# Queries of a recurrent-memory attention layer: copied and turned in two pieces of eight heads

## The chip, the cores and the metric

The kernel runs on one core of a Trainium2 chip. The metric is the device time of one execution in microseconds (us): for the kernel before, the median of three runs is 1795.13 us (1789.95, 1795.13 and 1798.88). Apart from these there is one execution taken by the hardware profiler, and all durations below come from that one.

The engines are named as in the profile: PE is the matrix engine (PEld its loading of weights), DVE is VectorE, ACT is ScalarE, POOL is GpSimd, and SP is the queue that starts most DMA transfers. L909 is line 909 of the kernel file.

## The reference

An input of 2048 rows of 1024 numbers is normalised; the result is the input, plus a dense layer with a GELU, plus an attention layer that goes through the rows in 64 segments of 32 tokens and carries 8 rows of memory from each segment to the next. The second part is the one that matters here:

```python
for s in range(n_seg):                       # 64 segments, one after the other
    xs = x[:, s * seg_len:(s + 1) * seg_len, :].copy()
    h = jnp.concatenate([mem, xs], axis=1)   # 8 rows of memory + 32 tokens
    q = jnp.einsum('btd,dhe->bhte', h, Wq)   # 32 heads of 128
    k = jnp.einsum('btd,dhe->bhte', h, Wk)
    v = jnp.einsum('btd,dhe->bhte', h, Wv)
    scores = jnp.einsum('bhqe,bhke->bhqk', q, k) * scale
    scores = jnp.where(mask[None, None], scores, -1000000000.0)
    p = _softmax(scores, axis=-1)
    o = jnp.einsum('bhqk,bhke->bhqe', p, v)
    o = jnp.einsum('bhte,hed->btd', o, Wo)
    mem = o[:, :M, :].copy()                 # M = 8, for the next segment
    outs.append(o[:, M:, :])
```

A segment can't begin before the memory of the one before is there, so the 64 segments form one long chain. The four weight matrices (1024 x 4096 each, in bf16) are too large to stay on the chip beside everything else.

## The kernel before

The first 405 us or so hold the normalisation and the dense layer. Then the loop over the 64 segments runs to the end (`for s in range(NSEG)`, line 803); the change lies in this loop alone.

**Weights.** The four matrices are cut into 64 units of 128 x 2048 numbers (512 KB). 47 of them lie in SBUF for the whole loop. 17 are brought in anew in every segment, through a ring of six buffers: 15 of these by DMA from DRAM (started from SP's queue at line 284 whenever `unit_done` says that a buffer is free), and two by VectorE out of PSUM, where they are kept (line 273).

**One segment on PE.** The order of work on each engine is the order in which the program is written; nothing is rearranged. PE goes through the passes K0, Q0, K1, Q1, V0, V1 (keys, queries and values of the two halves of 16 heads) and then O, the output product. A pass is eight units, one unit is four products of 32 rows by 512 columns side by side (line 830), and its sum goes to one PSUM bank. 24 of a segment's tokens and the 8 rows of memory are the 32 rows of these products. The other 8 tokens of each of four segments are gathered to a second set of 32 rows, the "left" rows, whose extra products fall on certain passes of certain segments. So the segments come in four kinds, by s modulo 4, which the code calls `i4`; `i4` = 1 and 3 have the more PE work, `i4` = 2 the least.

**Turning the queries.** A pass of queries leaves in its PSUM bank, for each of 16 heads, blocks of 32 tokens by 32 features. `turn_q` (line 906) has ScalarE copy them to SBUF as bf16 (line 909), into `q_home`, which has 40 columns a head: 8 for the left rows and 32 for these. Then VectorE turns each 32 x 32 block in its place (line 914, in the profile STREAM_TRANSPOSE `kq<-kq`). `q_left` (line 925) puts the left rows' queries into the first 8 columns of each head. `q_home` is the first 640 columns of `q_all`, a part of the tile `kq`.

**Who needs the turned queries.** `scores(u)` (products at line 947 for the own rows, at line 953 for the left rows) takes the turned queries and keys. `scores(0)` is written into PE's order after seven units of pass K1 (after six in segments with `i4` = 3), `scores(1)` after the first unit of V1 (after the second with `i4` = 3). If the turn isn't finished when PE comes there, PE waits, as do all units behind.

**The two calls differ.** Queries of the first half (`turn_q(psQ)`, line 1130) are copied whole, 512 columns in one instruction. For the second half (`turn_q(psQ1, (0, 10, 16))`, line 1151) the copy has two pieces, heads 0 to 9 and heads 10 to 15. The reason is in `exps(0)`, line 969: the probabilities of the first half are put into columns 400 to 623 of `q_all`, which is where heads 10 to 15 lie. They are read last at line 1024, in `sums(0)`. So the copy of heads 10 to 15 has to wait for line 1024, and that of heads 0 to 9 hasn't. The turn is one instruction over all 16 heads in both calls.

On VectorE's queue the order around the second call is line 1012, line 1024 (twice), line 925, line 914. On ScalarE's queue it is line 996, line 999 (twice), line 909 (twice), and then the copy of the values, line 886.

Of the kernel before, what the change touches and what calls it, by code (L numbers as in the profile page):

```python
# [38 lines left out]
NL = SEG - NX  # L39
# [81 lines left out]
def kernel(  # L121
# [16 lines left out]
    nc = tc.nc  # L138
# [60 lines left out]
    for j in range(4):  # L199
# [11 lines left out]
        out=m, in_=m, pattern=[[1, NX]], compare_op=ALU.is_ge, fill=0.0, base=0, channel_multiplier=-1,  # L211
    )
    for half in range(2):
        m = mask_left[0:SEG, :, 8 - 8 * half:16 - 8 * half]
        nc.gpsimd.affine_select(
            out=m, in_=m, pattern=[[-8, GRP], [0, 8]], compare_op=ALU.is_ge, fill=0.0, base=0, channel_multiplier=1,
        )
        nc.gpsimd.affine_select(
            out=m, in_=m, pattern=[[8, GRP], [1 if half else 0, 8]], compare_op=ALU.is_ge, fill=0.0,
# [91 lines left out]
    nat_home, q_home = d_oL[:, 0:512].rearrange("p (h t) -> p h t", h=16), q_all[:, 0:640].rearrange("p (h t) -> p h t", h=16)  # L311
# [29 lines left out]
    def new_ps(way="ps"):  # L341
        k = turns[way][0]
        turns[way].rotate(-1)
        shape, kind = ([P, 512], F32) if way == "ps" else ([P, KT, P], BF16)
        ps = banks.tile(shape, kind, name=way, tag=f"bank{k}")
        place_of[id(ps)] = k, ps
        return ps

    with tc.tile_pool(name="ma", bufs=2) as ma:
# [31 lines left out]
        for j in range(4):  # L381
            nc.sync.dma_start(
                out=o_sb[32 * j + NX:32 * j + 32, 0:8, :],
                in_=mem0[:, 256 * j:256 * j + 256].rearrange("m (h e) -> m h e", h=8),
# [200 lines left out]
        for tg in range(4):  # L585
# [18 lines left out]
            for fb in range(FC):  # L604
                if tg == 0 and fb < BEGUN:
                    ps = begun[fb]
                else:
                    ps = new_ps()
# [3 lines left out]
                    out=xb[:, :], in_=ps[:, :], func=ACT.Identity, bias=b1col[:, fb:fb + 1], scale=1.0  # L612
# [4 lines left out]
                    out=u[:, :], in0=u[:, :], scalar1=0.044715, scalar2=1.0, op0=ALU.mult, op1=ALU.add  # L617
# [18 lines left out]
            if tg == 0:  # L636
                for nb in range(2):
                    cs = slice(nb * 512, nb * 512 + 512)
                    ps = new_ps()
# [3 lines left out]
            if not last:  # L643
# [7 lines left out]
                for t in range(4):  # L651
# [6 lines left out]
                    for nb in range(2):  # L658
                        cs = slice(nb * 512, (nb + 1) * 512)
                        ps = new_ps()  # L660
# [21 lines left out]
            else:  # L682
# [32 lines left out]
                for step in range(FC + AHEAD):  # L715
                    for t in range(4):
# [3 lines left out]
                        for nb in range(2):  # L720
# [6 lines left out]
                            if add_at.get(fc + 1) == n:  # L727
                                ps, cs = pss[n], slice(512 * nb, 512 * nb + 512)
# [7 lines left out]
    with tc.tile_pool(name="late", bufs=1) as late:  # L736
# [15 lines left out]
        def let_go(ps):  # L752
            free_banks.append(bank_of.pop(id(ps))[0])
# [49 lines left out]
        for s in range(NSEG):  # L803
# [44 lines left out]
            def half_pass(w, u, left, at):  # L848


                ps = new_acc()
                now = [i for w_, i, u_ in units[:48] if (w_, u_) == (w, u)]
                psL, ahead, order = None, [], now
                if left and led and led["next"][:2] == (w, u):
                    psL, ahead, order = led["next"][2:]
                    assert led["made"] == len(ahead)
                    led.clear()
                elif left:
                    psL = new_acc()
                lag = LAG if first else 0  # L860
                tiles = {}
                for n in range(KT + lag):
                    if n < KT:
                        tiles[now[n]] = unit_tile((w, now[n], u))
                        product(w, now[n], tiles[now[n]], hT, ps, now)
                    if n < lag:
                        continue
                    i = now[n - lag]
                    t = tiles.pop(i)
                    if left and i not in ahead:  # L870
                        product(w, i, t, hL, psL, order)
                    if first and (w, i, u) == IN_PSUM:
                        for b in range(2):
                            keep(IN_PSUM, 1024 * b, t[:, 1024 * b:1024 * b + 1024], b)
                    unit_done((w, i, u))
                    for fn in at.get(n - lag, ()):
                        fn()
                return ps, psL
# [24 lines left out]
                kL[u] = left_keys[u]  # L903
                turn(ps, kL[u], nc.vector.tensor_copy if first else nc.scalar.copy)

            def turn_q(ps, cuts=(0, 16)):

                for h0, h1 in zip(cuts, cuts[1:]):
                    nc.scalar.copy(  # L909
                        out=q_home[:, h0:h1, NL:40], in_=ps[:, 32 * h0:32 * h1].rearrange("p (h e) -> p h e", e=32)  # L910
                    )
                let_go(ps)
                home = q_home[:, :, NL:40]
                nc.vector.transpose(out=home, in_=home)  # L914

            def turn_qL(ps, u):
                turn(ps, qL[u][:, :, :], nc.vector.tensor_copy)
# [1 line left out]
            def q_left(u):  # L919

                if i4 >= 2 + u and more:
                    q = qS[:, i4 - 2 - u, :, :]
                else:
                    q = qL[u][:, :, NL * i4:NL * i4 + NL]
                nc.vector.tensor_copy(out=q_home[:, :, 0:NL], in_=q)
# [201 lines left out]
            if first:  # L1127
                turn_qL(psQL, 0)
                q_left(0)
            turn_q(psQ)  # L1130
            if left_q[0] and not first:
                turn_qL(psQL, 0)
# [14 lines left out]
            psQ1, psQ1L = half_pass("Q", 1, left_q[1], at)  # L1147
            if first:
                turn_qL(psQ1L, 1)
                q_left(1)  # L1150
            turn_q(psQ1, (0, 10, 16))
            if left_q[1] and not first:
                turn_qL(psQ1L, 1)
            if not final:
# [45 lines left out]
            for n, unit in enumerate(O_UNITS):  # L1200
# [8 lines left out]
                if n == 6 and left_o:  # L1209
                    st["resL"] = pd_main[:, 0:256]  # L1210
                    loads.dma_start(
                        out=st["resL"], in_=resL_d[og, :, :]
# [104 lines left out]
```

## Time and profile before

| what | value | from |
|---|---|---|
| median of the runs | 1795.13 us | three runs |
| the profiled execution | 1796.11 us, its span 1794.4 us | its own time |
| PE busy | 1696.3 us, 95% of the span | page, part 1 |
| DVE busy | 983.8 us, 55% | page, part 1 |
| ACT busy | 683.6 us, 38% | page, part 1 |
| one copy L909 of 512, 320, 192 columns | 586, 429, 319 ns | groups by shape |
| one turn L914 of 512 columns | 711 ns, 128 of them | groups |

How to read it: the span is the time from the first to the last instruction of the profiled execution. "Busy" is the time in which an engine had an instruction under way; the ends of PE's products are modelled, and a product of 512 columns is shown as 380 ns though the next one starts some 215 ns after it, so that a short pause of PE can hide behind the shown end of the product before. The granted clock of PE was 1.000 over the whole execution. "DMA share" is the time that packets took, summed over the 16 DMA engines and divided by 16 times the stretch; it can be a little over 1 where packets overlap.

### The profile page before, as it was taken

What the parts mean: (1) busy time and instruction counts of PE and PEld (TensorE: products, weight loads), DVE (VectorE), ACT (ScalarE), POOL (GpSimd) and SP (SyncE); (2) the same over time, 40 slices, a digit from 0 to 9 for tenths busy, and PEclk for the clock granted to TensorE, in tenths of its full rate; (3) what the DMA queues carried; (4) which work ended last, traced back from release to release, by engine and by line L of the source; (5) the groups of instructions that cost most, each with busy time, mean ns of one, the idle gap of its engine ahead of it and who ended that gap; (6) DMA issues with size and microseconds to landing.
All of it is one profiled execution on the core that took longest, in us unless ns stands there. A gap on an engine that the chain in (4) does not pass through costs nothing.

```text
span 1794.4 us, 71508 instructions
## 1 busy us (share of the span) xinstructions
PE 1696.3 (95%) x31164; PEld 889.3 (50%) x31164; DVE 983.8 (55%) x2514; ACT 683.6 (38%) x1692; POOL 300.4 (17%) x586
## 2 busy tenths in 40 slices
PE   9999999999999999999999999999999989999988
PEld 5444444444555555545454555554545544554544
DVE  7656483825555555555455555555555554555544
ACT  6344251603333333334343434343434333433333
POOL 0000002301231111212122121121121111111111
PEclk9999999999999999999999999999999999999999
DMA  9455312789999999999999999999999999999998
GB/s 279 144 169 165 87 48 73 267 277 371 391 385 383 387 376 384 377 379 382 365 394 371 390 386 398 378 393 372 374 382 384 385 371 369 380 383 381 370 386 316
DMA packets 232830, 594.44 MB, mean 331 GB/s; under 512 B 57715, under 2 KB 88035, under 8 KB 232516
## 3 DMA queue, kind: packets, MB, share of 16 engines
q1 hardware_dynamic: 197584, 567.08, 84.4%
q0 software_dynamic: 16896, 16.85, 2.9%
q10 hardware_dynamic: 18036, 5.94, 1.3%
q8 instruction: 244, 4.00, 0.9%
q14 instruction: 70, 0.57, 0.1%
HBM read 573.43 MB, written 28.90 MB: 336 GB/s over the span
## 4 chain that ended last, share of the span: by engine, by line
PE 75%; DMA 11%; ACT 4%; DVE 4%; issue 4%; ACTq 1%; SPq 1%; POOL 0%; DVEq 0%; POOLq 0%
PE acc L830 38%; PE acc L1088 12%; PE ps L534 10%; DMA u<-Wc_O 8%; PE ps L662 6%; PE ps L693 3%; DMA u<-Wc_V 2%; ACT mixed L999 2%; PE acc L1039 1%; PE mixed L947 1%; DVE kq L914 1%; ACTq L459 1%; DVE pd_main L1012 1%; ACT kq L909 1%; SPq L521 1%
## 5 line engine op out<-in xcount | busy, mean ns | idle before, releaser
L830 PE MATMUL acc<-u,hr_home 128*32 128x512 bf16 x11520 | 758.8, 380 | 14.7 <-issue 8.3
L830 PEld LDWEIGHTS <-hr_home 128*32 128x32 bf16 x12288 | 350.3, 96 | 281.1 <-issue 33.2
L830 PE MATMUL acc<-u,hrL 128*32 128x512 bf16 x2880 | 256.2, 380 | 2.6 <-DVE qL L882 1.0
L534 PE MATMUL ps<-u 128*128 128x512 bf16 (+1 forms) x992 | 195.0, 358 | 0.0
L273 DVE TENSOR_SCALAR u<-kept 128x512 uint32<-128x512 uint32 x254 | 163.2, 684 | 56.9 <-PE acc L830 43.2
L1088 PE MATMUL acc<-u,d_oL 128*32 128x512 bf16 x2592 | 168.9, 380 | 13.1 <-issue 7.9
L882 ACT CAST d_oL<-acc 128x512 bf16<-128x512 f32 x143 | 82.0, 584 | 256.8 <-PE acc L830 251.5
L1088 PE MATMUL acc<-u,kq 128*32 128x256 bf16 (+1 forms) x2884 | 135.8, 310 | 13.6 <-DMA u<-Wc_O 11.2
L662 PE MATMUL ps<-u 128*128 128x512 bf16 x672 | 146.0, 379 | 0.0
L534 PEld LDWEIGHTS <-u 128*128 128x128 bf16 x992 | 91.6, 98 | 101.5
L1088 PEld LDWEIGHTS <-kq 128*32 128x32 bf16 x3908 | 103.0, 96 | 75.4 <-ACT kq L1058 21.2
L1012 DVE TENSOR_TENSOR pd_main<-kq,mixed 128x320 bf16<-128x320 bf16 x128 | 62.5, 488 | 130.2 <-ACT mixed L999 130.2
L914 DVE STREAM_TRANSPOSE kq<-kq 128x512 bf16<-128x512 bf16 x128 | 91.0, 711 | 73.2 <-ACT kq L909 71.0
L909 ACT CAST kq<-acc 128x512 bf16<-128x512 f32 (+2 forms) x192 | 85.4, 445 | 112.2 <-PE acc L830 82.6
L1279 POOL DMA_DIRECT2D out_dram<-hr_home x168 | 85.4, 516 | 221.7 <-DVE hr_home L1246 221.7
L886 ACT CAST kq<-acc 128x512 bf16<-128x512 f32 x128 | 75.2, 588 | 112.2 <-PE mixed L953 112.2
L830 PEld LDWEIGHTS <-hrL 128*32 128x32 bf16 x3072 | 87.9, 96 | 58.5 <-issue 7.6
L977 DVE TENSOR_TENSOR kq<-kq,mixed 128x96 bf16<-128x96 bf16 (+1 forms) x256 | 38.1, 190 | 125.8 <-ACT kq L967 72.6
L662 PEld LDWEIGHTS <-u 128*128 128x128 bf16 x672 | 65.5, 98 | 78.8 <-DVE u L619 0.4
L611 ACT ACTIVATE u<-ps,b1col 128x512 bf16<-128x512 f32 x112 | 76.5, 684 | 65.4 <-PE ps L534 62.3
L1088 PEld LDWEIGHTS <-d_oL 128*32 128x32 bf16 x2592 | 64.6, 96 | 67.7 <-issue 20.8
L999 ACT ACTIVATE mixed<-mixed,small_consts 128x160 f32<-128x160 f32 x256 | 94.2, 368 | 8.4
(126 smaller groups left out, 1911.2 us busy)
## 6 DMA issues: line engine op xcount, KB each, us to landing
u<-Wc_K SPq DMA_DIRECT2D x256, 512.0 KB
u<-Wc_V SPq DMA_DIRECT2D x256, 512.0 KB
u<-Wc_O SPq DMA_DIRECT2D x256, 512.0 KB
u<-Wc_Q SPq DMA_DIRECT2D x192, 512.0 KB
u<-in_B_w_dram SPq DMA_DIRECT2D x28, 512.0 KB
u<-in_A_Wq_dram SPq DMA_DIRECT2D x13, 512.0 KB
u<-in_A_Wv_dram SPq DMA_DIRECT2D x12, 512.0 KB
u<-in_A_Wk_dram SPq DMA_DIRECT2D x9, 512.0 KB
```

Source lines behind the costliest of these rows:

```text
L273: nc.vector.tensor_single_scalar(out=out, in_=in_, scalar=0, op=ALU.bitwise_or)
L534: nc.tensor.matmul(ps[:, SEG * s0:SEG * s1].rearrange("p (s t) -> p s t", t=SEG), lhsT=w1_sb[fb // 2][:, kt, (fb % 2) * P:(fb % 2 + 1) * P ...
L611: nc.scalar.activation(out=xb[:, :], in_=ps[:, :], func=ACT.Identity, bias=b1col[:, fb:fb + 1], scale=1.0)
L662: nc.tensor.matmul(ps[:, :], lhsT=gts[fc // 4][:, fc % 4, t * P:(t + 1) * P], rhs=w2_sb[fc // 2][:, fc % 2, cs], start=(fc == 0), stop=(fc ...
L830: nc.tensor.matmul(o, lhsT=lhs[:, i, :], rhs=m, start=(i == seq[0]), stop=(i == seq[-1]), tile_position=(0, 32 * j),)
L882: cp(out=out, in_=ps.rearrange("p (h e) -> p h e", e=32))
L909: nc.scalar.copy(out=q_home[:, h0:h1, NL:40], in_=ps[:, 32 * h0:32 * h1].rearrange("p (h e) -> p h e", e=32))
L914: nc.vector.transpose(out=home, in_=home)
L999: nc.scalar.activation(out=mixed[:, 160 * b:160 * b + 160], in_=mixed[:, 0:160], func=ACT.Exp, scale=-1.0, bias=off[:, b:b + 1],)
L1012: nc.vector.tensor_tensor(out=pdA.rearrange("p c b q -> p b c q"), in0=prA[:, None, :, :].to_broadcast([P, 2, 4, 40]), in1=dd, op=ALU.mult,)
L1088: nc.tensor.matmul(acc[r0:r0 + rows, 0:256 * len(blocks)], lhsT=lhsT, skip_group_check=True, rhs=o_columns(t, k, blocks), start=start, sto ...
L1279: loads.dma_start(out=out_flat[rows, 256 * j:256 * j + 256], in_=res[32 * j:32 * j + NX, :])
```

## The change

Both calls now copy and turn in two pieces of eight heads. For each piece ScalarE copies 256 columns, and VectorE turns them. The instructions alternate in the program (copy, turn, copy, turn), but the two engines have queues of their own, so that ScalarE's second copy can run beside VectorE's first turn. The bank is let go after both. For the first half of the queries one copy and one turn become two of each; for the second half the two copies change from 320 and 192 columns to 256 and 256, and one turn becomes two. The second piece, heads 8 to 15, holds all of columns 400 to 623, and so it is the piece that waits for line 1024.

```diff
-            def turn_q(ps, cuts=(0, 16)):
-
-                for h0, h1 in zip(cuts, cuts[1:]):
+            def turn_q(ps):
+
+                for h0, h1 in ((0, 8), (8, 16)):
                     nc.scalar.copy(
                         out=q_home[:, h0:h1, NL:40], in_=ps[:, 32 * h0:32 * h1].rearrange("p (h e) -> p h e", e=32)
                     )
+                    half = q_home[:, h0:h1, NL:40]
+                    nc.vector.transpose(out=half, in_=half)
                 let_go(ps)
-                home = q_home[:, :, NL:40]
-                nc.vector.transpose(out=home, in_=home)
...
-            turn_q(psQ1, (0, 10, 16))
+            turn_q(psQ1)
```

## The prediction

> **What bounds the kernel now.** I read the windows first, one for each kind of segment, in the middle of the loop (`i4` = 3, 0, 1, 2). After the length come busy time of PE, PEld, DVE, ACT and POOL, the granted clock, the DMA share and GB/s.
>
> ```profile
> 995.74:1016.58 20.84, 20.17 (x466) 11.30 (x465) 11.17 (x29) 9.04 (x24) 3.80 (x7) 1.00 0.99 378
> 1016.58:1037.49 20.91, 20.06 (x466) 11.08 (x466) 11.79 (x30) 8.35 (x23) 3.71 (x7) 1.00 1.02 395
> 1037.49:1059.49 22.00, 21.39 (x472) 10.93 (x472) 10.54 (x29) 7.71 (x21) 3.71 (x7) 1.00 1.01 392
> 1059.49:1079.35 19.86, 18.42 (x434) 10.35 (x433) 12.41 (x32) 7.86 (x22) 4.72 (x9) 1.00 1.01 381
> ```
>
> Two things are near their limit together. PE is busy for 80.04 of 83.61 us, and the DMA share is about 1. ACT and DVE have room. So a pause of PE costs time where PE is the later of the two, and nothing where PE then waits for a weight anyway. PE's waits, the second view, show both sorts:
>
> ```profile
> PE acc L1088 <- DMA u<-Wc_O: 16.1, 27, 1.6
> PE mixed L947 <- DVE kq L914: 12.9, 40, 0.5
> ...
> PE acc L830 <- DMA u<-Wc_V: 5.4, 10, 1.3
> ```
>
> The 12.9 us for the turn is too little, since the modelled end of the product before hides part of each pause. I took instead, over all segments, the time from the start of PE's last product before the scores to the first score product. It is 0.206 us where nothing is waited for. Medians for `i4` = 0, 1, 2, 3 are 0.206, 0.345, 0.358, 0.563 us at scores(0), and 0.190, 0.904, 0.687, 0.256 us at scores(1). In all six cases above 0.21 the score starts 0.053 us after the turn's end, so the turn (L914) is what ends the pause. Summed, the pauses are 9.9 us at scores(0) and 14.7 us at scores(1), 24.6 us in all; the change acts on the end of that turn.
>
> The third view is the timeline, scores(0) and then scores(1) of one segment each (start, length):
>
> ```profile
> 1000.23 0.59 ACT L909 CAST kq<-acc 128x512 bf16<-128x512 f32 x1 [1.19 <-PE acc L830]
> 1000.85 0.71 DVE L914 STREAM_TRANSPOSE kq<-kq 128x512 bf16<-128x512 bf16 x1 [0.95 <-ACT kq L909]
> 1001.61 0.20 PE L947 MATMUL mixed<-kq,d_oL 128*32 128x40 bf16 x4 [0.18 <-DVE kq L914]
> ```
>
> ```profile
> 1046.28 0.43 ACT L909 CAST kq<-acc 128x320 bf16<-128x320 f32 x1
> 1047.17 0.32 ACT L909 CAST kq<-acc 128x192 bf16<-128x192 f32 x1 [0.46 <-DVE d_oL L1024]
> ...
> 1047.17 0.20 DVE L925 COPY kq<-qL 128x128 bf16<-128x128 bf16 x1
> 1047.52 0.71 DVE L914 STREAM_TRANSPOSE kq<-kq 128x512 bf16<-128x512 bf16 x1 [0.15 <-ACT kq L909]
> ```
>
> In the first, copy and turn follow each other: 0.586 + 0.032 + 0.711 = 1.33 us from the copy's start to the turn's end. In the second, only the copy of 192 columns (0.319) stands between L1024 and the turn: 0.319 + 0.033 + 0.711 = 1.063 us.
>
> **The change, part by part.** Shapes it brings in that L909 and L914 don't show are priced from these rows and the gaps beside them:
>
> ```profile
> L1058 ACT CAST kq<-acc 128x256 bf16<-128x256 f32 x64 | 24.2, 378 | 0.0
> ...
> 1003.11 0.71 DVE L1138 STREAM_TRANSPOSE d_oL<-d_oL 128x512 bf16<-128x512 bf16 x1 [0.32 <-ACT d_oL L882]
> 1003.74 0.67 DVE L896 STREAM_TRANSPOSE d_oL<-d_oL 128x512 bf16<-128x512 bf16 x1
> ```
>
> - Copy of 256 columns: L1058's row has 0.378, and L909's 319, 429 and 586 ns lie on a line that gives 0.374 for 256. I take 0.375. Successive copies from PSUM overlap by 0.10 us (L1058: 0.213 then 0.378, the second 0.109 after the first's start), so the second ends at 0.375 - 0.10 + 0.375 = 0.65.
> - Turn of 256 columns: not in the trace, every turn has 512. Bounds: half of 711 (0.356) if all of it scales, 0.711 if none does. DVE's casts from PSUM fall by 0.93 ns a column from 512 (654) to 256 columns (415 ns), and at about one ns a column the turn has 0.18 of fixed cost; I take 0.445. The nearest row for two turns in succession is the one above: L896 starts 0.635 after L1138, 0.076 before its end. So a half occupies DVE for 0.37.
> - scores(0): first copy 0 to 0.375, first turn from 0.41, second turn from 0.78 (its copy, at 0.65 + 0.03, is earlier), end at 1.22. Against 1.33 it gains 0.11 us. Pauses of 0.14, 0.15 and 0.36 us (`i4` = 1, 2, 3) are there to take it; 47 segments by 0.107 = 5.0 us. With `i4` = 0 the turn already ends 0.34 us early.
> - scores(1), from L1024's end: L925 starts at once, the first turn may start 0.11 after it (the gap from L925 to a turn that needn't wait), the second 0.37 later at 0.49. Its copy, which grows from 192 to 256 columns, is ready at 0.375 + 0.033 = 0.41 and so is hidden by the first turn; without that cover it would cost 0.055. The end is at 0.93 instead of 1.063: gain 0.13. `i4` = 1 and 2: 32 by 0.13 = 4.2 us; `i4` = 3 has 0.05 to give, 15 by 0.05 = 0.75 us.
> - Added: 128 turns, each 0.10 of DVE time (0.37 + 0.445 - 0.711), and 64 copies. They end earlier than the old turn did, so what is behind them on DVE (L882 and L896 where left queries are turned, else L977) isn't later; DVE is idle about 1 us there. Banks are let go 0.06 later, while PE has eight units of the next pass ahead. No DMA and no queue of SP or POOL is touched.
>
> Gross gain: 5.0 + 4.2 + 0.75 = 10 us. With a half turn at 0.356 (interval 0.28) the same steps give 1.05 and 0.77, which takes nearly all of some pauses: 19 us. With 0.711 (interval 0.635) they lose 0.42 and 0.39 us a turn, 39 us.
>
> The Trainium skill speaks against the overlap: "VectorE: DVE Perf Modes", The DRAIN you can't avoid, says that the next operation can't start before the pipe has emptied, and that fewer operations are the remedy. By that the ends are 1.30 and 1.00, and the gross gain is about 4 us. The trace doesn't agree here, since L896 started 0.076 us before L1138's end.
>
> **What reaches the end.** Start-to-start pauses of PE ahead of units (L830, L1088) sum to 64 us, 27 us of it in segments with `i4` = 2, most in the O pass and ended by a weight's DMA. What is saved ahead of such a wait comes back in it. In the last twentieth of `i4` = 1, the DMA share is 0.78: the buffers are full there and PE is behind, so savings in that segment mostly stay. I take three quarters of `i4` = 1's 3.8 us, half of `i4` = 3's 2.5, and a sixth of `i4` = 2's 3.8: 2.9 + 1.2 + 0.6 = 4.7, say 4 us. The profiled execution goes from 1796.1 to 1792; it lies 1.0 us above the median, which makes the median 1791.
>
> **Rivals.**
> - All of it is kept. For: PE is busy 95%, and its waits for DMA in the list are short. Against: a DMA share of 1. Then 1795.1 - 10 = 1785. The Trainium skill ("Trace Analysis", Identifying the Most-Contended Engine) calls the occupancy of 16 DMA engines misleading, which is for this rival; the GB/s, 378 to 395 beside a highest slice of 398, are against it.
> - Nothing is kept, DMA sets the pace throughout: 1795. Against: the 0.78 above.
> - Slower, the half turn is dear. It decides from an interval of 0.42 us (0.41 + 0.42 + 0.50 = 1.33): at 0.55 for a half, scores(0) ends at 1.43 and scores(1) at 1.13, 47 by 0.10 + 48 by 0.07 = 8 us gross; at 0.711, 39 us. DMA waits swallow up to half, so 1799 to 1834. Against: no DVE row here has so flat a price.
> - Slower, the change doesn't do what it says: the second copy is made to wait for the first turn, both being in one tile. Then 0.41 + 0.445 + 0.03 + 0.375 + 0.03 + 0.445 = 1.73 against 1.33, and much the same at scores(1), some 37 us gross, 1813 to 1832. Against: the copy of 320 columns at 1046.28 runs before L925 at 1047.17, though it is written after it and both write `q_home`; waits go by columns, not tiles.
>
> **Numbers.** Forecast 45%, all kept 20%, nothing kept 15%, dear half turn 13%, false wait 7%. The likeliest is 1791 us. The range, 1782 to 1804, holds the first three cases and the cheaper part of the dear turn; it leaves out the 19 us end and the losses above 9 us. A change under 0.5% (9 us) can't be told from none. Faster by over that: most of "all kept" and a little of the forecast, 18%. Slower: the false wait and half of the dear turn with some scatter, 16%. Within: 66%.
>
> **What would show it.** L914 with 256 turns of about 0.445 us, 0.37 apart; L909 with 256 copies of 0.375; at scores(0) the end 1.22 after the copy's start, at scores(1) 0.93 after L1024. The pause sums fall from 24.6 to about 15 us while PE's waits for `u<-Wc` grow by some 5. I am wrong if a half turn costs over 0.5 us, if ACT's second copy starts after the first turn's end, or if DMA waits don't grow.

## The result, and the profile after

The changed kernel takes 1788.44 us (median of 20 runs, 1777.46 to 1794.88), the kernel before in the same comparison 1795.2 us (20 runs, 1784.61 to 1806.02). The ratio is 0.9964 with a 95% interval of 0.9948 to 0.9980: 6.8 us faster, within 0.5%. A second comparison, below among the experiments, gave 0.9991 (0.9964 to 1.0018). Weighted by their intervals the two make 0.9971, about 5 us, with some 2.5 us of uncertainty.

The profiled execution has a span of 1793.2 us. Its first part happened to be 6 us longer than in the profile of before (the first segment ends at 440.4 us instead of 434.4 us, and 4.7 us of this are there at 348 us already, ahead of any changed instruction), so the span says little; the loop from the end of the first segment to that of the 63rd took 1326.9 us, against 1334.0.

The groups of the two changed lines, by shape:

```profile
L909 ACT CAST kq<-acc 128x256 bf16<-128x256 f32 x256 | 89.0, 375 | 115.9 <-PE acc L830 84.4 <-DVE kq L1024 17.1 <-DVE d_oL L1024 14.5
L913 DVE STREAM_TRANSPOSE kq<-kq 128x256 bf16<-128x256 bf16 x256 | 98.2, 422 | 49.6 <-ACT kq L909 49.6
```

A copy of 256 columns takes 375 ns. The turn (now L913) is shown with a mean of 422 ns; apart, the first of two has a median of 445 ns ahead of scores(0), 437 ahead of scores(1), and the second 402. The timeline at scores(0) of a segment with `i4` = 3, and at scores(1) of one with `i4` = 1 (start, length; two instructions of one kind are merged to a row, x2):

```profile
999.14 0.65 ACT L909 CAST kq<-acc 128x256 bf16<-128x256 f32 x2 [1.19 <-PE acc L830]
999.54 0.77 DVE L913 STREAM_TRANSPOSE kq<-kq 128x256 bf16<-128x256 bf16 x2 [0.74 <-ACT kq L909]
1000.16 0.40 PE L947 MATMUL mixed<-kq,d_oL 128*32 128x40 bf16 x4
1000.38 0.20 PE L953 MATMUL mixed<-kq,d_oL 128*32 128x16 bf16 x4
```

```profile
1047.47 0.35 DVE L1024 TENSOR_TENSOR d_oL<-kq,mixed 128x64 bf16<-128x64 bf16 x2
1047.85 0.20 DVE L925 COPY kq<-qL 128x128 bf16<-128x128 bf16 x1
1047.86 0.37 ACT L909 CAST kq<-acc 128x256 bf16<-128x256 f32 x1 [0.52 <-DVE d_oL L1024]
1047.96 0.76 DVE L913 STREAM_TRANSPOSE kq<-kq 128x256 bf16<-128x256 bf16 x2
1048.45 0.52 PE L947 MATMUL mixed<-kq,d_oL 128*32 128x40 bf16 x4
```

In the first, the two turns begin 0.40 us after the start of the first copy, while the second copy still runs, and end at 1000.31, that is 1.17 us after the copy's start (1.33 before). In the second, both turns lie right behind L925 and end 0.86 us after the late copy's start (1.06 before). Over all segments the medians are 1.176 and 0.873 us.

The score products show something that the prediction hadn't. The first four of line 947 take 0.40 and 0.52 us instead of 0.20: two of the four belong to heads 0 to 7 and need only the first turn (they start 0.05 us after its end in the second view; in the first view PE comes later, 0.17 us after it), the other two wait for the second turn. So what is left of the pause lies inside the group of score products, and PE's list of waits no longer names the turn:

```profile
PE acc L1088 <- DMA u<-Wc_O: 20.8, 45, 1.5
PE acc L1088 <- issue: 8.7, 16, 1.4
PE acc L830 <- issue: 7.4, 14, 1.1
...
PE acc L830 <- DMA u<-Wc_V: 4.3, 8, 1.3
```

The 12.9 us of `L947 <- DVE kq L914` are gone, and the wait for the output weights has grown from 16.1 us (27 times) to 20.8 us (45 times). For the weights of all four matrices the list has 21.5 us before, 27.1 after and 28.4 in a second profile of the changed kernel (`after_again` below). To compare kernels in spite of the shifted pause I took from the trace's start times, for every segment from the ninth on, the time from PE's last unit before the scores to its first unit after them. Medians in us for `i4` = 0, 1, 2, 3; the last column is what exceeds 0.429 and 0.442 us, the medians for `i4` = 0 where nothing is waited for, times 16:

| kernel | at scores(0) | at scores(1) | pauses, us |
|---|---|---|---|
| before | 0.429, 0.550, 0.565, 0.769 | 0.441, 1.110, 0.892, 0.463 | 9.6 + 18.2 |
| after | 0.429, 0.429, 0.429, 0.606 | 0.446, 0.581, 0.689, 0.424 | 2.8 + 6.2 |

(The first row gives 27.8 where the prediction had 24.6, since it takes medians and all 16 segments of a kind.) One median is loose: at scores(1) with `i4` = 1 the segments of the changed kernel scatter from 0.45 to over 0.9 us, and the second profile gives 0.685 for the 0.581. Counted one by one, the pauses that end 0.03 to 0.08 us after a turn's end are 26.6 us before, and 10.5 and 8.1 in the two profiles of the changed kernel. So the pauses at the scores fell by 16 to 19 us, and the time by 5 to 7.

The difference is found again ahead of the weights. Pauses of over 0.09 us, start to start, ahead of the first product of a unit that is transferred anew rose from 28 us to 38 us in both profiles of the changed kernel. (Not counted are 0.19 us ahead of the ninth unit of the O pass in 47 segments, 9 us in all: there PE waits for ScalarE's copy of line 1058, also where that unit's transfer is left out.) The chain that ended last (share of the span) shows the same; before, DMA had 11% of it and PE 75%:

```profile
PE 73%; DMA 16%; issue 3%; DVE 3%; ACT 2%; ACTq 1%; SPq 1%; DVEq 0%; POOL 0%; POOLq 0%
```

### The profile page after: what moved, and what is told of

Read it like the earlier page. It is cut to its first block, busy times and chain, and to the rows that moved or that the text cites. A ratio compares the mean times of both kernels' runs of the same rounds, so it can differ in the third digit from the quotient of the medians.

```text
span 1793.2 us, 71764 instructions
## 1 busy us (share of the span) xinstructions
PE 1699.9 (95%) x31164; PEld 889.9 (50%) x31164; DVE 986.1 (55%) x2642; ACT 687.1 (38%) x1756; POOL 299.3 (17%) x586
## 4 chain that ended last, share of the span: by engine, by line
PE 73%; DMA 16%; issue 3%; DVE 3%; ACT 2%; ACTq 1%; SPq 1%; DVEq 0%; POOL 0%; POOLq 0%
PE acc L830 37%; PE acc L1088 12%; PE ps L534 10%; DMA u<-Wc_O 10%; PE ps L662 6%; DMA u<-Wc_V 4%; PE ps L693 3%; PE acc L1039 1%; ACT mixed L999 1%; ACTq L459 1%; PE mixed L947 1%; DMA u<-Wc_Q 1%; DVE pd_main L1012 1%; SPq L521 1%; PE mixed L953 1%
## 5 line engine op out<-in xcount | busy, mean ns | idle before, releaser
L830 PEld LDWEIGHTS <-hr_home 128*32 128x32 bf16 x12288 | 338.5, 96 | 291.1 <-issue 37.7
L830 PE MATMUL acc<-u,hrL 128*32 128x512 bf16 x2880 | 252.5, 380 | 4.0 <-issue 1.4
L273 DVE TENSOR_SCALAR u<-kept 128x512 uint32<-128x512 uint32 x254 | 163.3, 685 | 55.2 <-PE acc L830 38.0
L909 ACT CAST kq<-acc 128x256 bf16<-128x256 f32 x256 | 89.0, 375 | 115.9 <-PE acc L830 84.4
L913 DVE STREAM_TRANSPOSE kq<-kq 128x256 bf16<-128x256 bf16 x256 | 98.2, 422 | 49.6 <-ACT kq L909 49.6
```

Of the source, the lines that this page charges most:

```text
L273: nc.vector.tensor_single_scalar(out=out, in_=in_, scalar=0, op=ALU.bitwise_or)
L830: nc.tensor.matmul(o, lhsT=lhs[:, i, :], rhs=m, start=(i == seq[0]), stop=(i == seq[-1]), tile_position=(0, 32 * j),)
L909: nc.scalar.copy(out=q_home[:, h0:h1, NL:40], in_=ps[:, 32 * h0:32 * h1].rearrange("p (h e) -> p h e", e=32))
L913: nc.vector.transpose(out=half, in_=half)
```

## The experiments

Two questions were open: do both halves of the change act as worked out, through the overlap; and is it the transfers of weights that take back the rest of what PE saves? Ratios are to the kernel before, run on the same chip in the same call.

**One half of the change at a time.** In `first_only` the second call keeps its copies (0, 10, 16) and its one turn; in `second_only` the first call stays whole. `turn_q` takes the cuts of the copies there and, where a second list is given, the cuts of the turns, which then come behind all the copies; with one list each copy is followed by its turn. The calls of `first_only`:

```diff
-            turn_q(psQ)
+            turn_q(psQ, (0, 8, 16))
...
-            turn_q(psQ1)
+            turn_q(psQ1, (0, 10, 16), (0, 16))
```

> Two pieces for the first half of the queries alone; the second half is copied and turned as before. In the changed kernel's trace the second of the two turns ends 1.176 us after the first copy's start at scores(0), against 1.329 before: 0.153 earlier, of which the pauses of PE at scores(0) (0.14, 0.15 and 0.36 us for i4 = 1, 2, 3) can take 7 us over the loop. Theory (half of what PE saves comes back as waits for weights): the pauses at scores(0) fall from 10 to about 3 us, those at scores(1) stay near 15, and the time falls by 3 to 4 us, ratio 0.998. Rival 1 (everything is kept): 7 us, ratio 0.996. Rival 2 (the gain comes from the second half of the queries alone): no change, ratio 1.000.

> Two pieces for the second half of the queries alone (cut at head 8 instead of 10, two turns); the first half as before. In the changed kernel the second turn ends 0.873 us after the late copy's start, against 1.063 before: 0.19 earlier, and the pauses at scores(1) (0.70, 0.48, 0.05 us for i4 = 1, 2, 3) can take 7 us. Theory (half comes back as waits for weights): ratio 0.998, a gain of 3 to 4 us; pauses at scores(0) stay at 10 us. Rival 1 (everything is kept): ratio 0.996. Rival 2 (the gain comes from the first half alone): ratio 1.000.

Measured: `first_only` 1792.95 us, ratio 0.9996 (0.9971 to 1.0021), `second_only` 1792.51 us, ratio 0.9993 (0.9973 to 1.0013). Each holds the 0.998 that the theory asks for and each holds 1.000, so the times decide nothing but that neither half alone brings 0.996. The pauses are clear: 2.8 + 16.4 us in `first_only`, 9.6 + 4.4 in `second_only`, where before has 9.6 + 18.2. Each half removes the pauses of its own scores and nearly none of the other's.

**Copies in two pieces, the turn whole.** No turn can run beside a copy here.

```diff
-            turn_q(psQ)
+            turn_q(psQ, (0, 8, 16), (0, 16))
...
-            turn_q(psQ1)
+            turn_q(psQ1, (0, 8, 16), (0, 16))
```

> The copies cut at head 8 in both calls, but one turn over all 16 heads in each, so no turn runs beside a copy. Theory (the gain is the overlap of the first turn with the second copy): the turn ends later than before, at scores(0) by 0.06 us (the second copy ends 0.647 after the first one's start against 0.586) and at scores(1) by 0.055 (a late copy of 256 columns instead of 192); gross 0.06 by 47 and 0.055 by 48, 5 us, half of it kept: 1 to 3 us slower, ratio 1.000 to 1.002, with the PE's pauses up by 5 us. Rival (smaller copies alone bring the gain, for instance by freeing ScalarE or the bank): ratio 0.996.

Measured: 1794.7 us, ratio 0.9986 (0.9968 to 1.0004). The rival's 0.996 lies outside. The small loss that was expected (1.000 to 1.002) can't be seen. The stages got longer as worked out, at scores(0) by 0.06 us for `i4` = 1, 2 and 3, at scores(1) by 0.05 and 0.04 for `i4` = 2 and 3; with `i4` = 1, the loose median, it was 0.11 shorter. So without the overlap the pauses stay (12.5 + 17.9 us), and it is the overlap that takes them away. Pauses ahead of transferred units were 33 us in `first_only`, 37 in `second_only` and 32 here, against 28 before; since this kernel saves nothing, some 4 us of such a difference are scatter between executions.

**The second turn delayed.**

```diff
                     nc.vector.transpose(out=half, in_=half)
+                    if h0 == 0:
+                        for _ in range(3):
+                            q_left(u)
```

> The changed kernel with three more copies on VectorE (line 925's copy repeated, same numbers again) between the first and the second turn of each call, so that the second turn ends some 0.33 us later; nothing else differs. It measures how much of a delay of the turn reaches the end. Gross: at scores(0) 0.29, 0.30 and 0.33 us for i4 = 1, 2, 3, at scores(1) 0.33, 0.33 and 0.18, sixteen times each: 28 us. Theory (half is swallowed by waits for weights): 14 us over the changed kernel, ratio to the kernel before 1.004. Rival 1 (everything reaches the end): 28 us over the changed kernel, ratio 1.012. Rival 2 (weights set the pace, nothing reaches the end): ratio 0.996 as in the changed kernel.

Measured: 1812.71 us, ratio 1.0084 (1.0064 to 1.0104). The dose was larger than meant, as VectorE's timeline shows:

```profile
1049.80 0.45 DVE L913 STREAM_TRANSPOSE kq<-kq 128x256 bf16<-128x256 bf16 x1 [1.37 <-ACT kq L909]
1050.17 0.61 DVE L928 COPY kq<-qL 128x128 bf16<-128x128 bf16 x3
1050.70 0.44 DVE L913 STREAM_TRANSPOSE kq<-kq 128x256 bf16<-128x256 bf16 x1
```

The second turn starts 0.90 us after the first instead of 0.37. Each of the three copies writes the same columns and starts 0.03 us after the end of the one before, so they don't overlap. The pauses at the scores rise from 9 to 70 us; the time rises by 0.0113 of 1795 us over the changed kernel (1.0084 - 0.9971), 20 us. A third reaches the end. The pauses ahead of transferred units fall from 38 to 12 us: when PE is later, weights are there. So both rivals, all and nothing, are out, and of a delay about the same part arrives as of the gain.

**Fewer transfers, three of fifteen left out.** The core of the edit (the same in both kernels of the pair):

```diff
+SPARED = tuple([unit for unit in ORDER if IS_STREAMED[unit] and unit[0] == w and unit not in KEPT][-1] for w in "KVO")
...
             nonlocal used
+            if unit in SPARED:
+                return res_tiles[STANDS_IN[unit]]
```

> The kernel before with three of the seventeen streamed units of each segment (one each of keys, values and output) not brought in: PE multiplies by the tile of a unit that stays in SBUF, so these products use wrong weights, and 12 instead of 15 transfers of 512 KB run a segment. Nothing else changes on PE, DVE or ACT. It is the base of the next run. All theories: the waits for weights (64 us of PE pauses ahead of lines 830 and 1088 before) fall to under 20 us, the DMA share falls to about 0.85, and the time falls by 30 to 60 us.

> The changed kernel with the same three units of each segment not brought in (wrong weights for them, 12 transfers a segment), to be compared with the run before in this list. Theory (what the change saves on PE is swallowed by waits for weights): with these waits gone, nearly all that the earlier turns can give is kept: 7 us at scores(0) and 7 us at scores(1), 12 to 15 us faster than the light kernel before. Rival 1 (the missing half is lost to something else on PE, ACT or DVE): still 6 to 7 us. Rival 2 (the gain comes from another kind of transfers' timing): none.

Measured: `light_before` 1756.9 us, ratio 0.9801 (0.9770 to 0.9833), `light_after` 1751.23 us, ratio 0.9765 (0.9736 to 0.9795): 5.7 us apart, uncertain by some 5 us (estimated from the scatter of the six runs of each), not the 12 to 15 that the theory asked for. The DMA share was still 0.90 between 500 and 1700 us, and yet the waits for weights were gone: in neither profile does a pause of over 0.09 us stand ahead of a transferred unit, apart from the 0.19 us ahead of the ninth unit of the O pass, and PE's list names no transfer from `Wc`. What the list has at the lines of the units (830 and 1088 before, 835 and 1093 here) is marked "issue", which means that the profile shows nothing that was waited for, in `light_before`

```profile
PE acc L1093 <- issue: 8.9, 10, 1.9
PE acc L835 <- issue: 4.0, 10, 0.8
```

and in `light_after`

```profile
PE acc L835 <- issue: 10.4, 11, 2.0
PE acc L1093 <- issue: 9.1, 16, 1.0
```

The pauses at the scores fell by 14 us here (27.8 to 14.2), while pauses inside a unit, ahead of any product but its first, grew from 12 to 20 us (both without the first segment). In the two profiles there are 45 of these, and 43 of them end 1.1 to 1.7 us after the end of a 16 KB packet on the queue that the profile names "instruction"; of moments taken at random one in ten does. 13 of the 20 in `light_before` stand at the same unit of the same segment in `light_after`. So PE most likely waits for its own code there; no run tests that by itself. Eight profiles of kernels with all transfers have 14 to 22 us of such pauses, so with one profile each it stays open whether the change makes them grow.

The pair thus speaks against the theory in its narrow form, that waits for weights alone swallow the rest: without any, 6 us were kept, and 12 lie at the edge of the scatter. The next expectations call the waits still there, from a count of pauses near a landing; `light_before` has a record of a landing every 0.1 us, and so nearness shows no wait. A pair with less traffic was needed either way.

**Ten of fifteen left out.** As above, with another list:

```diff
+SPARED = tuple(unit for n, unit in enumerate([u for u in ORDER if IS_STREAMED[u] and u not in KEPT]) if n % 3)
```

> The kernel before with ten of the fifteen transferred units of each segment not brought in (a resident unit's tile takes their place, so their products use wrong weights): 5 transfers of 512 KB a segment. With three spared the DMA share fell only to 0.90 and pauses ended by a landing weight stayed (17 us in the light kernel before, 29 us in the light changed one), so that pair didn't take the waits away. Here the share should be near 0.45 and such pauses under 3 us. All theories: faster than the light kernel (0.980), ratio 0.960 to 0.970; the pauses at the scores stay at some 28 us.

> The changed kernel with the same ten units of each segment not brought in. Theory (waits for weights swallow half of what the earlier turns save): with these waits gone the whole fall of the pauses at the scores, 28 to 14 us, is kept: 13 to 15 us faster than the lighter kernel before, a ratio lower by 0.0075 to 0.0085. Rival (something on PE, ACT or DVE loses the other half): 6 to 7 us, a ratio lower by 0.0035.

Measured: `lighter_before` 1827.9 us, ratio 1.0179 (1.0145 to 1.0214), `lighter_after` 1822.91 us, 1.0155 (1.0124 to 1.0186). With a third of the transfers the kernel got slower, and the 5 us between the two are neither the 13 to 15 nor the 6 to 7 that were expected. VectorE's timeline of `lighter_before` shows why:

```profile
1019.35 0.34 DVE L1029 TENSOR_TENSOR kq<-kq,mixed 128x64 bf16<-128x64 bf16 x2
1019.72 0.22 DVE L930 COPY kq<-mixed 128x128 bf16<-128x128 bf16 x1
1019.87 1.28 DVE L275 TENSOR_SCALAR u<-kept 128x512 uint32<-128x512 uint32 x2
1021.06 0.70 DVE L919 STREAM_TRANSPOSE kq<-kq 128x512 bf16<-128x512 bf16 x1
```

The spared units gave up their turns in the ring of buffers, and so the refill of a kept unit by VectorE (L273 before, L275 here, 1.28 us) moved to just ahead of the turn for scores(1), whose stage grew to 2.06 us for `i4` = 1. In that place two turns are dearer than one: 0.76 us on VectorE instead of 0.70, since nothing but VectorE sets their end, and the stage at scores(1) grew by 0.05 us while that at scores(0) gained as ever. The pauses went from 9.6 + 64.3 to 2.8 + 66.4 us, down by 4.7, and the 5 us are all of that: at a DMA share of 0.41 nothing was swallowed.

**Ten left out, the ring's turns kept.** The spared unit takes its buffer and passes it on, without a transfer; VectorE's order is that of the kernel before.

```diff
-        unit, t = streams[n], slab(slot)
+        unit = streams[n]
+        if unit in SPARED:
+            stream_tiles[n], slot_of[n] = res_tiles.get(STANDS_IN[unit]), slot
+            return
+        t = slab(slot)
```

> The kernel before with the same ten transfers of each segment left out (resident tiles in their place, wrong weights), but each spared unit keeps its turn in the ring of buffers, so that VectorE's copies of the two kept units stay where they were in its order. In the last pair they had moved: a copy of 1.28 us stood right ahead of the turn for scores(1), and VectorE, not ScalarE, set the turn's end. All theories: DMA share near 0.41, hardly any pause ended by a landing weight, pauses at the scores 28 us as before, ratio 0.950 to 0.975.

> The changed kernel with the same ten transfers left out and the ring's turns kept. Theory (waits for weights swallow half of what the earlier turns save): pauses at the scores fall from 28 to 14 us, and with no such waits all of it is kept: 12 to 15 us faster than the run before in this list, a ratio lower by 0.007 to 0.0085. Rival (the other half is lost on PE, ACT or DVE): 6 to 7 us, a ratio lower by 0.0035.

Measured: `slots_before` 1721.11 us (1720.58 to 1724.81), ratio 0.9599 (0.9564 to 0.9634), `slots_after` 1706.41 us (1704.57 to 1709.04), ratio 0.9516 (0.9481 to 0.9550). The change is worth 14.7 us here, and no run of the one comes near the other. The pauses fell from 9.6 + 18.3 to 2.8 + 11.5 us, that is by 13.6. Between 500 and 1700 us the DMA share was 0.45, and PE's list of waits names no transfer of weights; its first lines in `slots_before`:

```profile
PE mixed L954 <- DVE kq L921: 17.1, 49, 0.8
PE acc L1046 <- DVE pd_main L1019: 8.0, 31, 0.3
```

and in `slots_after`, where the turn has left the list and nothing took its place:

```profile
PE acc L1046 <- DVE pd_main L1019: 8.0, 31, 0.3
PE acc L1046 <- ACT kq L889: 7.0, 15, 0.5
```

The windows from 500 to 1700 us (length, busy time of PE, PEld, DVE, ACT, POOL, clock, DMA share, GB/s), first of the changed kernel, then of `slots_after`:

```profile
500.00:1700.00 1200.00, 1130.74 (x25480) 614.73 (x25476) 646.62 (x1777) 463.47 (x1315) 225.70 (x427) 1.00 1.00 383
```

```profile
500.00:1700.00 1200.00, 1174.19 (x27116) 637.59 (x27108) 677.08 (x1887) 494.98 (x1403) 232.01 (x439) 1.00 0.45 146
```

The change is the same and takes away 14 us of pauses: at a DMA share of 0.45 all of it is kept, at 1.00 a third to a half. So the rival (6 to 7 us) is out, since a loss on PE, ACT or DVE would show here too, and so is rival 2 of the first pair, a change in the transfers' timing as the source of the gain. What swallows the rest comes with the transfers. This pair alone doesn't tell waits for weights from the pauses inside units, because both are gone here (none of either, the first segment apart). In the full kernel it is the pauses ahead of transferred units that grew, from 28 to 38 us, while those inside units were 22 us before and 15 and 19 us after.

**The changed kernel again, and one unit later.** `scores_later` is the changed kernel with one number changed:

```diff
-SCORES_0 = (6, 6, 6, 5)
+SCORES_0 = (6, 6, 6, 6)
```

> The changed kernel once more, beside the same runs of the kernel before as the other runs here: ratio 0.996 again if 6.8 us is the gain; a ratio of 0.998 or above would say that the first comparison was lucky, and that the two halves alone (0.9996 and 0.9993, each uncertain by 0.0025) add up to what there is.

> The changed kernel with scores(0) one unit later in segments with i4 = 3 (after seven units as in the other kinds, not six). There a pause of 0.18 us is left at scores(0) in the changed kernel. Theory: the unit of 0.215 us fills the pause, 16 by 0.18 = 2.8 us gross, half of it kept: 1 to 2 us below the changed kernel, not to be told from none by time, but the median stage at scores(0) with i4 = 3 falls from 0.606 to 0.43 us. Rival: the chain behind scores(0) (exponentials, sums, late copy) moves 0.04 us later and gives it back at scores(1), whose stage with i4 = 3 grows above 0.424 us.

Measured: `after_again` 1790.91 us, ratio 0.9991 (0.9964 to 1.0018). The interval overlaps the first one's and reaches from a gain of 6 us to a loss of 3; the first comparison lay on the lucky side, and I hold to the two together. `scores_later` 1789.17 us, ratio 0.9976 (0.9951 to 1.0001). The stage at scores(0) with `i4` = 3 fell from 0.605 to 0.456 us and that at scores(1) stayed at 0.425, so the rival is out (0.43 had been expected at scores(0)), but the time can't be told from the changed kernel's. No version here is shown to beat the changed kernel.

## Why the prediction was right

**The pauses and what ends them.** Right: in all six cases the turn's end had set PE's start, and moving it moved PE, in full where no transfer interfered (14.7 us in the `slots` pair).

**Copy and turn of 256 columns.** Predicted 0.375, measured 0.375 and 0.372 to 0.377. First turn predicted 0.445, measured 0.445; the second starts 0.369 (scores(0)) and 0.36 (scores(1)) after it, predicted 0.37. The second turn was mis-sized: 0.402 instead of 0.445, because an instruction right behind another of its kind is shown shorter, which L896 behind L1138 (0.67 against 0.71) had already told; in `delayed`, with copies between, the second turn takes 0.436. So the ends are 1.176 and 0.873 us, not 1.22 and 0.93, and the gains a turn 0.153 and 0.19, not 0.11 and 0.13, and a pair of turns costs VectorE 0.06 us more than the one turn (98.2 against 91.0 us of busy time for 128), not 0.10.

**The gross gain.** Predicted 10 us, measured 14 by the medians without interference (`slots`): the error is the 0.05 to 0.06 us by which each turn's gain was put too small, and nothing else in the sum. With the measured ends the same sum gives 7 + 7 us. Counted one by one the pauses fell by 16 us in the `slots` pair (31.0 to 15.0) and by 16 and 18.5 us in the full kernel; the 19 us of the medians there rest in part on the loose one.

**What reaches the end.** Predicted 4.7 of 10, measured 5 (with 6.8 in the first comparison) of 14 to 16. That more than half comes back as waits was right, and the waits ahead of transferred units did grow: by 6 to 7 us in PE's list, where some 5 were predicted, and by 10 us from start to start. That it comes with the transfers is shown by the `slots` pair, and that it acts both ways by the delay, of which a third arrived. That the number fits so well is in part luck, since the gross gain was put too small and the part that is kept, 47%, rather too large. The reading behind that part was also too simple: of the 64 us of pauses ahead of units, taken as mostly waits for weights, 28 stand ahead of a transferred unit, 9 are the pause ahead of the ninth unit of the O pass, ended by ScalarE's copy, and 24 lie inside units, where PE most likely waits for its code.

The split over the kinds of segment is only partly borne out: means over single executions give 23.11 to 22.59 us for `i4` = 1 and 21.53 to 21.29 for `i4` = 3, nothing for `i4` = 2 (20.30 to 20.26), as predicted, and `i4` = 0, which was to stay, got longer, 21.11 to 21.46; in the second profile of the changed kernel it didn't (21.03), and there `i4` = 3 gained only 0.1 (21.44). With so few profiles that stays open.

**The rivals.** "All is kept" was wrong because of the transfers, as said. "Nothing is kept" is excluded for the full kernel by the first comparison and by the two taken together, not by the second alone. The dear half turn and the false wait didn't come: the second copy started 0.27 us after the first, while no turn was done. The rule of the Trainium skill ("VectorE: DVE Perf Modes", The DRAIN you can't avoid) that the next operation starts only after the pipe has emptied would have put the second turn 0.445 us after the first; the trace has 0.369. The same section adds that a next operation which isn't held starts earlier; the trace fits that, and the prediction left it out. The other rule of the Trainium skill ("Perfetto Trace Analysis", Identifying the Most-Contended Engine), that the occupancy of the DMA engines misleads, is half borne out: the share of 1.00 went with savings that were swallowed and 0.45 with savings that were kept, but at 0.90 no pause stood ahead of a transferred unit any more.

## What to carry to other kernels

When two engines work one after the other on one block and a third waits for the end, splitting the block in two hides the shorter work behind the longer for the price of one more start on each, here 0.06 us of VectorE against 0.15 to 0.19 us earlier; it pays only while the first engine's wait leaves the second idle, and behind a busy VectorE the same split cost 0.06 us. Before counting on the gain, see what else runs at its limit: with PE busy 95% and a DMA share of 1.00, a third to a half of the saving was kept. To find out how much is swallowed, take the second resource's load away without moving anything else in the queues; the delay of a known size is the cheaper test, and it agreed, with a third. To find out by what, count the pauses by what they stand ahead of: nearness in time to a transfer shows nothing where transfers are always under way.

## What was not expected

The time's scatter is smaller with fewer transfers. The 20 runs of the kernel before lie 1.2% apart (1784.61 to 1806.02) and those of the changed one 1.0%; with a third of the transfers the four to six runs of one kernel lie within 0.3% (1704.57 to 1709.04). The pauses inside units, 14 to 22 us in the full kernels' profiles, are gone there; whether they make the scatter isn't shown. A change of a few us is measured far better in the kernel with less traffic, but there it has another size.

Taking work away made the kernel slower: with ten transfers fewer and the ring's order changed, 1827.9 us, with the order kept, 1721.11 us. The two differ in whether the spared units take their turn in the ring, and what this moves on VectorE is the place of the kept units' refills (1.28 us each, two a segment): PE's start-to-start pauses ahead of the scores and of the memory rows' product (line 320 before) were some 75 and 64 us with the order changed, some 30 and 9 us with it kept.
